# An attention and two-layer mixer kernel whose first token tile gets a written-out order

## Chip, cores and metric

The kernel runs on one core of one Trainium2 chip. The metric is the device time of one execution in microseconds; the time of a kernel is the median of its runs.

## The reference

Attention over 4 batches, 8 heads and a head width of 64: 512 local queries per head see the keys within 32 positions and 32 global keys, and 32 global queries see all 544 keys. The result, 4 x 544 = 2176 tokens of width 512, passes through two layers. The first multiplies by w_in (512 x 2048), applies a piecewise function that is 0 below -1, a parabola between -1 and 1 and the identity above, and multiplies by w_out. The second multiplies the tokens by w_a and w_b (512 x 1536 each), takes the product of the two element by element and multiplies by its own w_out. Cut to what matters here:

```python
s_l = concat([scale * q_l @ k_g.T, where(|i - j| <= 32, scale * q_l @ k_l.T, -1e9)])
e = exp(s - max(s)); a = e / (sum(e) + 1e-9)
x = (a @ v).transpose(0, 2, 1, 3).reshape(tokens, 512)
h = x @ w_in
g = where(h >= 1, h, where(h <= -1, 0, (h + 1) ** 2 / 4))
x = g @ w_out
out = (x @ w_a) * (x @ w_b) @ w_out2
```

## The kernel before

Tokens are cut into 17 blocks of 128 and these into six tiles t (`TILES`), of three blocks each but the last. Attention works on items: one block of 128 queries and one pair of heads p. An item loads `qk` (queries, then the keys of its window, L169) and `v` (L179). Three items make a group (`Local`, L191); in tile 0 a group is one pair p for all three blocks, so groups 0 to 3 give the four column chunks of x of that tile. A group runs through these steps:

- scores on TensorE (PE), `s_pe` L198, 24 products of 64x32 pieces into two PSUM tiles;
- mask and negated row maximum on VectorE (DVE), L215, and exp on ScalarE (ACT), L220. For tiles after the first the exp also adds up its rows;
- `norm` L223: row sums (for tile 0 by a reduction, L226), 1e-9, reciprocal of 128x6, and the six 128x128 pieces scaled, half on ScalarE (L230), half on DVE (L231);
- `t_pe` L233: transposes by a product with `ident`, copied to `pt` by ScalarE (L239);
- `v_pe` L241: 24 products with the values into `o`, copied to `xraw` by DVE (L259).

`x_chunk` (L348) splits a chunk of x into a rounded high part xh (ScalarE, L355) and the rest xl (DVE, L356). Every product of the layers is made of three: high weight by high x (L519), low weight by high x (L520), high weight by low x (L521).

`h_unit(t, f)` (L839) makes 12 such products for 128 columns f of w_in into `hp`, after which ScalarE makes r (L858) and DVE and ScalarE make g in two parts. `x_unit(t, f)` (L868) multiplies g by the rows f of w_out into four sums, two units later. h0 to h5 below are the units of tile 0 in the first stage (six of its sixteen units, `FA`); then tile 1 runs through all of its units, then tile 0 through the rest. Attention of later tiles is cut into small steps (`atoms`) that are put between the units.

Weights arrive as raw 64-bit floats (`w_load` L96, 512 KB each) and are converted: one step on ScalarE (L110), two on DVE (L111, L112), then a split on ScalarE (L119) and DVE (L120). `W1` streams them in the order i0, i1, o0, i2, o1, i3, ... (i for w_in, o for w_out). The pool `wp` has 32 slots of 4 KB per partition, shared by the first twelve `qk` and `v` tiles, the raw weights named in `EARLY` and later the converted weights; other raw tiles go through a pool of two.

The order at the start: `EARLY` fixes the loads on SP's queue (k for an item's `qk`, v for its values, w for a raw weight). Tile 0 is written as steps (`piece` L434, `tpose` L457) with filler products (`fill`, L186) between them, 54 of them, and one weight conversion behind every fifth step. The instructions of all engines are then put in order by the scheduler of the tile framework, which also places steps of later groups between those of earlier ones. During the first stage, `LEAD1` says how many weights are converted ahead of unit f.

Of the kernel before, what the change touches and what calls it, by code (L numbers as in the profile page):

```python
# [9 lines left out]
F32 = mybir.dt.float32  # L10
# [8 lines left out]
P = 128  # L19
# [33 lines left out]
START_ATOMS = 5  # L53
LEAD1 = 4

PAIRS = [(0, 1), (4, 5), (2, 3)]
NF = 12
# [12 lines left out]
def body(tc, qk, vw, kg, vg, vt, w1i, w1o, w2a, w2b, w2o, mask, eye, out):  # L70
# [10 lines left out]
    ident = cp.tile([P, P], F32, name="ident")  # L81
    half = cp.tile([P, 1], F32, name="half")
    nc.gpsimd.memset(half, 0.5)
    masks = ap.tile([P, 3, P], BF16, name="masks", bufs=1)

    def f32(t):
# [104 lines left out]
    class Local:  # L191
        def __init__(self, t, members):
            self.t = t
            self.tag = "h" if t else "acc"
            self.items = members
            self.nt = len(members)

# [8 lines left out]
                                         start=True, stop=True, tile_position=(64 * h, WIN * a))  # L206

        def s_post(self):
            self.e = ap.tile([P, 3, 2, P], F32, name="e", tag="e", bufs=EBUFS)
            mn = ap.tile([P, 3, 2], F32, name="mn", tag="mn", bufs=EBUFS)  # L210
            self.sm = ap.tile([P, 3, 2], F32, name="sm", tag="sm", bufs=EBUFS)
            for n, it in enumerate(self.items):
                m = 1 if it.i == 0 else (2 if it.i == SL // P - 1 else 0)
                for h in range(2):
                    nc.vector.tensor_tensor_reduce(  # L215
                        self.e[:, n, h], self.s[h][:, n], masks[:, m], -SCALE, 3.0e38, ALU.add, ALU.min,
                        mn[:, n, h:h + 1])
                for h in range(2):
                    acc = self.sm[:, n, h:h + 1] if self.t else None
                    nc.scalar.activation(self.e[:, n, h], self.e[:, n, h], AF.Exp, bias=mn[:, n, h:h + 1],  # L220
                                         scale=-1.0, accum_out=acc)

        def norm(self):  # L223
            sm = self.sm[:, :self.nt]
            if not self.t:
                nc.vector.tensor_reduce(sm, self.e[:, :self.nt], mybir.AxisListType.X, ALU.add)  # L226
            nc.vector.tensor_scalar_add(sm, sm, 1e-9)
            nc.vector.reciprocal(sm, sm)
            for n in range(self.nt):
                nc.scalar.activation(self.e[:, n, 0], self.e[:, n, 0], AF.Copy, scale=self.sm[:, n, 0:1])  # L230
                nc.vector.tensor_scalar_mul(self.e[:, n, 1], self.e[:, n, 1], self.sm[:, n, 1:2])  # L231

        def t_pe(self, n):  # L233
            it = self.items[n]
            tp = ps.tile([P, 2, P], F32, name="tp", tag=self.tag)
            for h in range(2):
                nc.tensor.transpose(tp[:, h], self.e[:, n, h], ident)
            it.pt = ap.tile([P, 2, P], F32, name="pt", tag="pt", bufs=PTBUFS)
            nc.scalar.activation(it.pt, tp, AF.Copy)  # L239

        def v_pe(self):  # L241
            self.o = ps.tile([P, self.nt * P], F32, name="o", tag=self.tag)
            for n, it in enumerate(self.items):
                for a in range(NQ):
                    for h in range(2):
                        r = slice(64 * h, 64 * h + 64)
                        q0 = WIN * a
                        nc.tensor.matmul(self.o[r, n * P + q0:n * P + q0 + WIN], it.v[:, a, r],  # L248
                                         it.pt[:, h, q0:q0 + WIN], start=True, stop=True)

        def v_post(self):
# [93 lines left out]
    def widths(t):  # L345
        return P * len(TILES[t])
# [86 lines left out]

    def piece(gs, gv):  # L434
        def run():
            if gs == 0:
                for kind in EARLY:
                    {"k": load_k, "v": load_v, "w": lambda: W1.load_to(W1.li + 1)}[kind]()
            else:
                loads()  # L440
            if gs is not None:
                if gs > START_GROUPS:
                    groups[gs - 1].norm()
                s_part(groups[gs])
            if gv is not None:
                v_part(groups[gv])
            if 0 < (gs or 0) < START_GROUPS:
                fill(WARM_S)
            if gv is not None:
                groups[gv].v_post()  # L450
                if groups[gv].t == 0:
                    x_chunk(0, groups[gv].items[0].p, widths(0))
            if gs is not None:
                groups[gs].s_post()
        return run

    def tpose(g, n):  # L457
        def run():
            loads()
            if n == 0 and (g < START_GROUPS or g == len(groups) - 1):  # L460
                groups[g].norm()
            groups[g].t_pe(n)
            if g < START_GROUPS:
                fill(WARM_T)
        return run

    atoms = [piece(0, None), piece(1, None)]
    ends = {}
    ns = 2
    for g, grp in enumerate(groups):  # L470
        n = grp.nt if isinstance(grp, Local) else 1
        atoms += [tpose(g, i) for i in range(n)]
        hold = g == START_GROUPS - 2
        atoms.append(piece(None if hold or ns >= len(groups) else ns, g))
        ns += not hold
        if grp.t >= 0:
            ends[grp.t] = len(atoms)
        if g == START_GROUPS - 1:
            atoms.append(piece(ns, None))
            ns += 1  # L480
    ends[len(TILES) - 1] = len(atoms)
    done = {"n": 0}

# [346 lines left out]
    ws2 = [(("y", f2), w2o[f2]) for f2 in range(NF2)]  # L830
# [75 lines left out]
    for u in range(len(units)):  # L906
        for kind in (0, 1):
            if kind == 0:
# [362 lines left out]
```

## Time and profile before

| | |
|---|---|
| median of 3 runs | 901.22 us (901.16 to 906.14) |
| profiled execution | 902.52 us, its span 900.7 us |
| granted clock of TensorE, mean | 0.996 |
| busy share of the span | PE 98%, DVE 70%, ACT 54% |
| moved by DMA | 153.61 MB, mean 171 GB/s |

The span runs from the first to the last instruction of the profiled execution; 1.8 us lie around it. Times in the rows count from the span's start. PE is the matrix engine's products, PEld its weight loads; a product of two 32-bit operands stands as two passes (x2) where its operands are not of the rounded type. Busy PE includes fillers. "Granted clock" 1.00 is 2.4 GHz.

### The profile page before, as it was taken

How to read it: one execution, taken by the hardware profiler on the slowest of the kernel's cores; microseconds unless marked ns; L12 is line 12 of the kernel's file. 1: busy time of each engine (PE TensorE's matmuls, PEld its weight loads, DVE VectorE, ACT ScalarE, POOL GpSimd, SP SyncE). 2: the span in 40 equal slices, each digit the busy share in tenths (PEclk: the TensorE clock that was granted, in tenths of full speed). 3: DMA queues.
4: the chain of work that ended last, by engine and by line, in shares of the span. 5: the costliest groups of instructions: out<-in, count | busy, mean ns of one | idle time of the engine just before them, and what ended most of it. 6: DMA issues, size and time to landing. Idle time of an engine off the chain costs nothing.

```text
span 900.7 us, 19419 instructions
## 1 busy us (share of the span) xinstructions
PE 884.2 (98%) x7382; PEld 837.8 (93%) x7382; DVE 634.3 (70%) x1587; ACT 489.2 (54%) x1192; POOL 0.3 (0%) x5
## 2 busy tenths in 40 slices
PE   8999998999999999999999999999999999999998
PEld 7889997999999999988999999999988999999998
DVE  5779897666566655555489687776987568676683
ACT  5869675555455444443456555555755446555442
POOL 0000000000000000000000000000000000000000
PEclk9999999999999999999999999999999999999999
DMA  9787566755543532344283454432788421644521
GB/s 324 241 280 259 179 217 220 268 180 187 161 139 131 173 113 90 121 146 150 74 283 85 149 194 155 164 118 109 245 293 278 152 82 42 200 136 132 198 102 54
DMA packets 82413, 153.61 MB, mean 171 GB/s; under 512 B 9488, under 2 KB 40592, under 8 KB 82320
## 3 DMA queue, kind: packets, MB, share of 16 engines
q1 hardware_dynamic: 81744, 151.85, 51.5%
q8 instruction: 58, 0.95, 0.4%
q10 hardware_dynamic: 576, 0.52, 0.2%
q14 instruction: 35, 0.29, 0.1%
HBM read 119.05 MB, written 33.29 MB: 169 GB/s over the span
## 4 chain that ended last, share of the span: by engine, by line
PE 84%; DMA 7%; DVE 4%; ACT 3%; issue 1%; SPq 0%; ACTq 0%; DVEq 0%
PE hp L519 6%; PE acc L519 6%; PE hp L521 6%; PE hp L520 6%; PE acc L520 6%; PE acc L521 6%; PE pb L712 4%; PE pb L714 4%; PE pb L715 4%; PE o L248 3%; PE px L712 3%; PE py L779 3%; PE px L714 3%; PE px L715 3%; PE py L780 3%; PE py L778 3%
## 5 line engine op out<-in xcount | busy, mean ns | idle before, releaser
L519 PE MATMUL hp<-xh,w 128*128 128x384 f32 (+1 forms) x384 | 132.2, 344 | 4.4 <-ACT pt L239 1.7
L519 PE MATMUL acc<-g,w 128*128 128x384 f32 (+1 forms) x384 | 127.7, 333 | 0.0
L521 PE MATMUL hp<-xl,w 128*128 128x384 f32 (+1 forms) x384 | 126.4, 330 | 0.4 <-DMA xl<-x0d 0.4
L520 PE MATMUL hp<-xh,w 128*128 128x384 f32 (+1 forms) x384 | 126.2, 329 | 0.0
L520 PE MATMUL acc<-g,w 128*128 128x384 f32 (+1 forms) x384 | 125.7, 327 | 0.0
L521 PE MATMUL acc<-g,w 128*128 128x384 f32 (+1 forms) x384 | 125.7, 327 | 0.0
L859 DVE SCALAR_TENSOR_TENSOR m<-hp,r 128x384 f32<-128x384 f32 (+1 forms) x96 | 51.2, 533 | 85.5 <-ACT r L858 85.3
L858 ACT ACTIVATE r<-hp,half 128x384 f32<-128x384 f32 (+1 forms) x96 | 53.9, 561 | 89.8 <-PE hp L521 86.5
L863 ACT ACTIVATE g<-m 128x384 fp32r<-128x384 f32 (+1 forms) x96 | 48.4, 504 | 58.6 <-DVE m L860 58.5
L519 PEld LDWEIGHTS hp<-xh,w 128*128 128x128 f32 x384 | 72.8, 190 | 7.0 <-ACT pt L239 2.0
L712 PE MATMUL pb<-w 128*128 128x384 f32 (+1 forms) x240 | 78.1, 325 | 1.2 <-ACT r L751 0.6
L119 ACT ACTIVATE w<-wt 128x512 fp32r<-128x512 f32 (+1 forms) x94 | 53.6, 571 | 46.4 <-PE pb L715 27.5
L714 PE MATMUL pb<-w 128*128 128x384 f32 (+1 forms) x240 | 78.2, 326 | 0.0
L715 PE MATMUL pb<-w 128*128 128x384 f32 (+1 forms) x240 | 78.0, 325 | 0.0
L521 PEld LDWEIGHTS hp<-xl,w 128*128 128x128 f32 x384 | 72.8, 190 | 1.3 <-DMA xl<-x0d 1.0
L519 PEld LDWEIGHTS acc<-g,w 128*128 128x128 f32 x384 | 72.4, 188 | 0.9
L520 PEld LDWEIGHTS hp<-xh,w 128*128 128x128 f32 x384 | 73.1, 190 | 0.0
L521 PEld LDWEIGHTS acc<-g,w 128*128 128x128 f32 x384 | 72.4, 188 | 0.2
L520 PEld LDWEIGHTS acc<-g,w 128*128 128x128 f32 x384 | 72.4, 189 | 0.0
L864 DVE TENSOR_TENSOR g<-m,g 128x384 fp32r<-128x384 f32 (+1 forms) x96 | 51.1, 533 | 22.4 <-ACT g L863 22.2
L120 DVE TENSOR_TENSOR w<-wt,w 128x512 fp32r<-128x512 f32 (+1 forms) x94 | 57.8, 617 | 4.0 <-ACT w L119 2.9
L220 ACT ACTIVATE e<-e,mn 128x128 f32<-128x128 f32 x128 | 48.0, 394 | 13.1 <-DVE mn L215 13.1
(169 smaller groups left out, 2063.0 us busy)
## 6 DMA issues: line engine op xcount, KB each, us to landing
v<-in_vw_dram SPq DMA_DIRECT2D x64, 256.0 KB, 5.2
wt<-wd SPq DMA_DIRECT2D x50, 256.0 KB, 2.9
qk<-in_qk_dram SPq DMA_DIRECT2D x62, 176.0 KB, 4.2
wraw<-in_w1i_dram SPq DMA_DIRECT2D x16, 512.0 KB, 4.9
wraw<-in_w1o_dram SPq DMA_DIRECT2D x16, 512.0 KB, 4.4
wraw<-in_w2a_dram SPq DMA_DIRECT2D x12, 512.0 KB, 4.3
wraw<-in_w2b_dram SPq DMA_DIRECT2D x12, 512.0 KB, 3.7
wd<-wt SPq DMA_DIRECT2D x24, 256.0 KB, 2.3
```

The costliest lines, as they stand in the source:

```text
L119: nc.scalar.activation(hi, src, AF.Copy)
L120: nc.vector.tensor_tensor(lo, src, f32(hi), ALU.subtract)
L519: nc.tensor.matmul(acc, whi, xhi, start=first, stop=False)
L520: nc.tensor.matmul(acc, wlo, xhi, start=False, stop=False)
L521: nc.tensor.matmul(acc, whi, xlo, start=False, stop=last)
L712: nc.tensor.matmul(out[:, :n], w[:, 0, r], hi[:, c, :n], start=start and c == 0, stop=False, skip_group_check=True)
L714: nc.tensor.matmul(out[:, :n], w[:, 1, r], hi[:, c, :n], start=False, stop=False, skip_group_check=True)
L715: nc.tensor.matmul(out[:, :n], w[:, 0, r], lo[:, c, :n], start=False, stop=k in (1, 5, 6) and c == 1, skip_group_check=True)
L858: at["act"] = nc.scalar.activation(r[:, :W], hp[:, :W], AF.Relu, bias=half, scale=0.5 / W_UP).ins
L859: nc.vector.scalar_tensor_tensor(m[:, :W], hp[:, :W], 1.0 / W_UP, r[:, :W], ALU.mult, ALU.max)
L863: nc.scalar.activation(gh[:, :W], m[:, :W], AF.Copy)
L864: nc.vector.tensor_tensor(gl[:, :W], m[:, :W], f32(gh[:, :W]), ALU.subtract)
```

## The change

Tile 0 leaves the steps and is written out in `begin`. Under `in_order` each of PE, ScalarE and DVE runs its instructions of `begin` in the order in which they are written; SP is not bound. The rows of a group are no longer scaled before the transposes. Instead, six products of `pt` with a tile of ones give each column's sum in the layout of `o` (`z`), and `v_post` adds 1e-9, takes the reciprocal of 128x384 and multiplies `o` by it. The fillers go from 54 to 16. `EARLY` is longer: two more key tiles, five more value tiles and four more raw weights, so that eight raw weights lie in slots of `wp`. Conversions of three weights are spread over groups 1 to 3 (`w_begin`, `w_end`). `LEAD1` is 3 instead of 4, and the conversions of the first stage are `paced`, that is, put behind the last h unit's r and g on ScalarE and DVE.

```diff
-WARM_S, WARM_T = 6, 3
+WARM = 4
-EARLY = "kkkkkkkkkvvvkkkwvvvwvvvwkkkvvvw"
+EARLY = "kkkkkkkkkvvvkkkwvvvwvvvwkkkvvvwkkvvvwwvvww"
-LEAD1 = 4
+LEAD1 = 3
...
         def norm(self):
             sm = self.sm[:, :self.nt]
-            if not self.t:
-                nc.vector.tensor_reduce(sm, self.e[:, :self.nt], mybir.AxisListType.X, ALU.add)
...
         def v_pe(self):
-            self.o = ps.tile([P, self.nt * P], F32, name="o", tag=self.tag)
+            self.o = ps.tile([P, self.nt * P], F32, name="o", tag="h")
...
+            if not self.t:
+                self.z = ps.tile([P, self.nt * P], F32, name="z", tag="h")
+                for n, it in enumerate(self.items):
+                    for h in range(2):
+                        nc.tensor.matmul(self.z[64 * h:64 * h + 64, n * P:(n + 1) * P], ones, it.pt[:, h],
+                                         start=True, stop=True)
...
         def v_post(self):
...
-                nc.vector.tensor_copy(xraw_cur[self.t][it.p][:, it.j * P:(it.j + w) * P],
-                                      self.o[:, n * P:(n + w) * P])
+                x = xraw_cur[self.t][it.p][:, it.j * P:(it.j + w) * P]
+                c = slice(n * P, (n + w) * P)
+                if self.t:
+                    nc.vector.tensor_copy(x, self.o[:, c])
+                else:
+                    z = mp.tile([P, 384], F32, name="zs", tag="r", bufs=3)
+                    nc.vector.tensor_scalar_add(z, self.z[:, c], 1e-9)
+                    nc.vector.reciprocal(z, z)
+                    nc.vector.tensor_tensor(x, self.o[:, c], z, ALU.mult)
...
+    def w_begin():
+        pend.append(w_conv())
+        W1.si += 1
+        W1.load_to(W1.si + sp["raw"])
+
+    def w_end():
+        key, tf = pend.pop(0)
+        w = slot()
+        split(w[:, 0], w[:, 1], tf)
+        wslots[key] = w
...
+    def begin():
+        for kind in EARLY:
+            {"k": load_k, "v": load_v, "w": lambda: W1.load_to(W1.li + 1)}[kind]()
+        n = START_GROUPS
+        s_part(groups[0])
+        groups[0].s_post()
+        s_part(groups[1])
+        fill(WARM)
+        for g in range(n):
+            for i in range(3):
+                groups[g].t_pe(i)
+                if g + 1 < n:
+                    groups[g + 1].post(i)
+            if g + 2 < n:
+                s_part(groups[g + 2])
+            if pend:
+                w_end()
+            v_part(groups[g])
+            if g + 1 < n:
+                fill(WARM)
+            else:
+                s_part(groups[n])
+            groups[g].v_post()
+            x_chunk(0, g, widths(0))
+            if g:
+                w_begin()
+        groups[n].s_post()
+        while pend:
+            w_end()
...
-    att_step(10 ** 9)
-    k = 0
-    while att_step(ends[0]):
-        k += 1
-        if k % START_ATOMS == 0:
-            W1.step()
+    with in_order():
+        begin()
...
                     while W1.si < min(2 * f + LEAD1, n1):
-                        W1.step()
+                        paced(W1.step)
                 if si == 1:
-                    want = max(n1 + (len(ws1) - n1) * (f + 1) // (NF1 - 3), 2 * f + LEAD1)
+                    want = max(n1 + (len(ws1) - n1) * (f + 1) // (NF1 - 3), 2 * f + LEAD1 + 1)
```

What stands on the engines at three places (a row: line, operation, tile written <- tiles read, shape, count). First ScalarE in tile 0, between the splits of chunk 0 (`xh0`) and chunk 1 (`xh1`); in the kernel before `e_439` and `e_560` belong to groups 2 and 3, `pt_473` to `pt_491` to group 1:

```order
L355 ACTIVATE xh0_435<-xraw0_398 128x384
L220 ACTIVATE e_439<-e_439,mn_440 128x128
L239 ACTIVATE pt_473<-tp_470 128x256
L239 ACTIVATE pt_482<-tp_479 128x256
L239 ACTIVATE pt_491<-tp_488 128x256
L230 ACTIVATE e_439<-e_439,sm_441 128x128 x3
L110 ACTIVATE wt_675<-wraw0_217 128x512
L220 ACTIVATE e_560<-e_560,mn_561 128x128 x5
L355 ACTIVATE xh1_556<-xraw1_399 128x384
```

In the changed kernel, the same stretch; `pt_437` to `pt_458` belong to group 1, `e_439` to group 2, `wt_535` is the first weight:

```order
L371 ACTIVATE xh0_430<-xraw0_385 128x384
L242 ACTIVATE pt_437<-tp_434 128x256
L225 ACTIVATE e_439<-e_439,mn_440 128x128 x2
L242 ACTIVATE pt_449<-tp_446 128x256
L225 ACTIVATE e_439<-e_439,mn_440 128x128 x2
L242 ACTIVATE pt_458<-tp_455 128x256
L225 ACTIVATE e_439<-e_439,mn_440 128x128 x2
L371 ACTIVATE xh1_531<-xraw1_386 128x384
L111 ACTIVATE wt_535<-wraw0_203 128x512
```

The scalings (L230) are gone, and exp and copies alternate behind xh0; the next xh stands directly behind them, with the conversion of a weight behind it.

Second, DVE in tile 0. Before, from the copy of group 0's `o` on (`sm_441` are the row sums of group 2):

```order
L259 COPY xraw0_398<-o_402 128x384
L215 ISA e_439,mn_440<-s1_373,masks_75 128x128
L215 ISA mn_440 128x1
L111 TENSOR_SCALAR wt_593<-wt_593 128x512
L356 TENSOR_TENSOR xl0_436<-xraw0_398,xh0_435 128x384
L226 TENSOR_REDUCE sm_441<-e_439 128x6
L112 SCALAR_TENSOR_TENSOR wt_593<-wraw0_209,wt_593 128x512
L227 TENSOR_SCALAR sm_441<-sm_441 128x6
L228 RECIPROCAL sm_441<-sm_441 128x6
L231 TENSOR_SCALAR e_439<-e_439,sm_441 128x128 x3
```

In the changed kernel, from the sums of group 1 on (`e_544` are the masks of group 3):

```order
L274 TENSOR_SCALAR zs_527<-z_515 128x384
L275 RECIPROCAL zs_527<-zs_527 128x384
L276 TENSOR_TENSOR xraw1_386<-o_490,zs_527 128x384
L372 TENSOR_TENSOR xl1_532<-xraw1_386,xh1_531 128x384
L112 TENSOR_SCALAR wt_535<-wt_535 128x512
L113 SCALAR_TENSOR_TENSOR wt_535<-wraw0_203,wt_535 128x512
L220 ISA e_544,mn_545<-s0_464,masks_77 128x128
```

The copy became three instructions (L274 to L276), and they, xl and two steps of a conversion (L112, L113) stand ahead of the next group's masks, which stood ahead of the copy before.

Third, ScalarE around r of unit h0 (`r_786` before, `r_740` now). Before:

```order
L110 ACTIVATE wt_843<-wraw_682 128x512
L110 ACTIVATE wt_852<-wraw_771 128x512
L858 ACTIVATE r_786<-hp_773,half_73 128x384
L230 ACTIVATE e_749<-e_749,sm_751 128x128 x3
L220 ACTIVATE e_828,sm_830<-e_828,mn_829 128x128
L863 ACTIVATE g_788<-m_787 128x384
L220 ACTIVATE e_828,sm_830<-e_828,mn_829 128x128 x5
L119 ACTIVATE w_847<-wt_843 128x512
L119 ACTIVATE w_856<-wt_852 128x512
L858 ACTIVATE r_876<-hp_861,half_73 128x384
```

In the changed kernel, where `wt_797` and `w_801` are the weight of h2:

```order
L111 ACTIVATE wt_705<-wraw0_219 128x512
L913 ACTIVATE r_740<-hp_727,half_73 128x384
L111 ACTIVATE wt_797<-wraw0_233 128x512
L111 ACTIVATE wt_804<-wraw0_245 128x512
L225 ACTIVATE e_709,sm_711<-e_709,mn_710 128x128 x6
L120 ACTIVATE w_724<-wt_705 128x512
L225 ACTIVATE e_782,sm_784<-e_782,mn_783 128x128
L233 ACTIVATE e_709<-e_709,sm_711 128x128 x3
L225 ACTIVATE e_782,sm_784<-e_782,mn_783 128x128 x5
L120 ACTIVATE w_801<-wt_797 128x512
L120 ACTIVATE w_808<-wt_804 128x512
L918 ACTIVATE g_742<-m_741 128x384
```

The weight of h2 was converted ahead of r before; `w_847` and `w_856` there are for later units. Now its conversion begins behind r, and twelve exp of groups 4 and 5 with three scalings stand between that and its split. Before, six of those twelve exp stood ahead of r.

On SP's queue the third key tile of group 5 (`qk_746`), which the end of h0 has to wait for in PE's row, now stands behind two more raw weights and six stores of x0 (`x0_store` L498), of which the last reads xl2.

## Rows read from the trace of the kernel before

**Rows 1.** The page's busy table: busy us (share of span) xinstructions of each engine.

```profile
PE 884.2 (98%) x7382; PEld 837.8 (93%) x7382; DVE 634.3 (70%) x1587; ACT 489.2 (54%) x1192; POOL 0.3 (0%) x5
```

**Rows 2.** Timeline of PE: start, us, engine line op out<-in xcount [idle before <-releaser].

```profile
12.28 0.80 PE L205 MATMUL s<-qk 64*32 64x128 f32 x20 [2.81 <-DMA qk<-in_qk_dram]
...
44.38 0.42 PE L519 MATMUL hp<-xh,w 128*128 128x384 f32 x1
...
53.85 0.64 PE L519 MATMUL hp<-xh,w 128*128 128x384 f32 x1 [1.70 <-ACT pt L239]
...
63.06 0.44 PE L519 MATMUL hp<-xh,w 128*128 128x384 f32 x1
```

**Rows 3.** The chain that ended last, 0 to 60 us: start us, us, what.

```profile
16.82 0.67 PE warm L189 x6
17.49 1.52 PE o L248 x48
...
35.88 1.52 PE o L248 x48
...
37.77 0.17 PE hp L520
...
54.49 0.32 PE hp L520
```

**Rows 4.** Timeline of ScalarE (ACT), columns as in rows 2.

```profile
6.21 3.62 ACT L220 ACTIVATE e<-e,mn 128x128 f32<-128x128 f32 x12 [2.31 <-DVE mn L215]
...
40.88 0.58 ACT L858 ACTIVATE r<-hp,half 128x384 f32<-128x384 f32 x1 [0.66 <-PE hp L521]
41.35 0.97 ACT L230 ACTIVATE e<-e,sm 128x128 f32<-128x128 f32 x3
```

**Rows 5.** Windows of 5 us: length, busy by engine, granted clock, DMA share, GB/s.

```profile
10.00:15.00 5.00, 2.72 (x30) 2.46 (x31) 2.21 (x8) 1.61 (x5) 0.00 (x0) 0.80 0.96 316
...
20.00:25.00 5.00, 5.00 (x101) 4.68 (x100) 4.27 (x19) 3.60 (x12) 0.00 (x0) 1.00 1.04 367
```

**Rows 6.** Tile v: two issues on SP (6.0 to 7.5 us), and landing.

```profile
L184 SPq DMA_DIRECT2D v<-in_vw_dram x2: 328/379/430, 6.1 to 6.5; - x2
...
DMA to landing us min/median/max: 4.9/5.1/5.2
```

**Rows 7.** Groups of DVE by shape: names, shapes, count, busy us, mean ns, idle.

```profile
L112 DVE SCALAR_TENSOR_TENSOR wt<-wraw,wt 128x512 int32<-128x512 int32 x68 | 46.8, 689 | 1.2
...
L215 DVE CUSTOM_DVE_ANT_0 e<-s,masks 128x128 f32<-128x128 f32 x128 | 30.0, 286 | 7.3 <-PE s L205 7.0 <-PE tp L237 0.3
L111 DVE TENSOR_SCALAR wt<-wt 128x512 int32<-128x512 int32 x68 | 28.7, 423 | 15.3 <-ACT wt L110 15.3
...
L887 DVE TENSOR_SCALAR x<-acc 128x384 f32<-128x384 f32 x10 | 5.5, 555 | 2.3 <-PE acc L521 2.2
...
L228 DVE RECIPROCAL sm<-sm 128x6 f32<-128x6 f32 x20 | 3.8, 190 | 0.6
...
L227 DVE TENSOR_SCALAR sm<-sm 128x6 f32<-128x6 f32 x20 | 3.4, 170 | 7.8 <-ACT e L220 7.7
...
L228 DVE RECIPROCAL sm<-sm 128x4 f32<-128x4 f32 x2 | 0.4, 178 | 0.1
L227 DVE TENSOR_SCALAR sm<-sm 128x4 f32<-128x4 f32 x2 | 0.3, 171 | 0.4 <-ACT e L220 0.4
```

**Rows 8.** Groups of ScalarE by shape, columns as in rows 7.

```profile
L220 ACT ACTIVATE e<-e,mn 128x128 f32<-128x128 f32 x128 | 48.0, 394 | 13.1 <-DVE mn L215 13.1
...
L110 ACT ACTIVATE wt<-wraw 128x512 f32<-128x512 f32 x68 | 45.0, 665 | 16.4 <-DMA wraw<-in_w1o_dram 7.6 <-DVE w L120 7.0 <-DMA wraw<-in_w1i_dram 1.7
L119 ACT ACTIVATE w<-wt 128x512 fp32r<-128x512 f32 x69 | 43.2, 628 | 18.9 <-DVE wt L112 11.1 <-PE px L715 6.4 <-PE acc L521 0.9
...
L239 ACT ACTIVATE pt<-tp 128x256 f32<-128x256 f32 x64 | 24.0, 378 | 6.6 <-PE tp L237 6.2 <-ACT w L119 0.3
...
L355 ACT ACTIVATE xh<-xraw 128x384 fp32r<-128x384 f32 x20 | 10.5, 526 | 1.9 <-DVE xraw L259 1.8
```

More of the change, by code (lines that the diff above doesn't have):

```diff
@@ L83, in body @@
     nc.gpsimd.memset(half, 0.5)
+    ones = cp.tile([P, D], F32, name="ones")
+    nc.gpsimd.memset(ones, 1.0)
     masks = ap.tile([P, 3, P], BF16, name="masks", bufs=1)
@@ L193, in __init__ @@
             self.t = t
-            self.tag = "h" if t else "acc"
             self.items = members
@@ L208, in s_post, with post @@
         def s_post(self):
[L209 to L221, printed above, removed]
+            for n in range(self.nt):
+                self.post(n)
+        def post(self, n):
+            if n == 0:
+                self.e = ap.tile([P, 3, 2, P], F32, name="e", tag="e", bufs=EBUFS)
+                self.mn = ap.tile([P, 3, 2], F32, name="mn", tag="mn", bufs=EBUFS)
+                self.sm = ap.tile([P, 3, 2], F32, name="sm", tag="sm", bufs=EBUFS)
+            i = self.items[n].i
+            m = 1 if i == 0 else (2 if i == SL // P - 1 else 0)
+            for h in range(2):
+                nc.vector.tensor_tensor_reduce(
+                    self.e[:, n, h], self.s[h][:, n], masks[:, m], -SCALE, 3.0e38, ALU.add, ALU.min,
+                    self.mn[:, n, h:h + 1])
+            for h in range(2):
+                acc = self.sm[:, n, h:h + 1] if self.t else None
+                nc.scalar.activation(self.e[:, n, h], self.e[:, n, h], AF.Exp, bias=self.mn[:, n, h:h + 1],
+                                     scale=-1.0, accum_out=acc)
         def norm(self):
             sm = self.sm[:, :self.nt]
-            if not self.t:
-                nc.vector.tensor_reduce(sm, self.e[:, :self.nt], mybir.AxisListType.X, ALU.add)
             nc.vector.tensor_scalar_add(sm, sm, 1e-9)
@@ L234, in t_pe @@
             it = self.items[n]
-            tp = ps.tile([P, 2, P], F32, name="tp", tag=self.tag)
+            tp = ps.tile([P, 2, P], F32, name="tp", tag="h" if self.t else "acc")
             for h in range(2):
@@ L249, in v_pe @@
                                          it.pt[:, h, q0:q0 + WIN], start=True, stop=True)
+            if not self.t:
+                self.z = ps.tile([P, self.nt * P], F32, name="z", tag="h")
+                for n, it in enumerate(self.items):
+                    for h in range(2):
+                        nc.tensor.matmul(self.z[64 * h:64 * h + 64, n * P:(n + 1) * P], ones, it.pt[:, h],
+                                         start=True, stop=True)
         def v_post(self):
@@ L435, in run @@
         def run():
[L436 to L440, printed above, removed]
+            loads()
             if gs is not None:
-                if gs > START_GROUPS:
-                    groups[gs - 1].norm()
+                groups[gs - 1].norm()
                 s_part(groups[gs])
@@ L459, in run @@
             loads()
-            if n == 0 and (g < START_GROUPS or g == len(groups) - 1):
+            if n == 0 and g == len(groups) - 1:
                 groups[g].norm()
             groups[g].t_pe(n)
-            if g < START_GROUPS:
-                fill(WARM_T)
-        return run
-    atoms = [piece(0, None), piece(1, None)]
-    ends = {}
-    ns = 2
+        return run
+    pend = []
+    def w_begin():
+        pend.append(w_conv())
+        W1.si += 1
+        W1.load_to(W1.si + sp["raw"])
@@ new lines, in w_end, with in_order @@
+    def w_end():
[3 more added lines that the diff above has]
+        wslots[key] = w
+    @contextlib.contextmanager
+    def in_order():
+        traced = nc.cur_bb.bb.instructions
+        n0 = len(traced)
+        yield
+        last = {}
+        for i in traced[n0:]:
+            if i.engine in (mybir.EngineType.PE, mybir.EngineType.Activation, mybir.EngineType.DVE):
+                if i.engine in last:
+                    tc.add_manual_dep(
+                        i, last[i.engine].name,
+                        mybir.DependencyInfo(mybir.DependencyClass.NoSync, mybir.DependencyReason.DATA),
+                        reason="in_order")
+                last[i.engine] = i
@@ L470, in body @@
+    atoms = [piece(START_GROUPS + 1, None)]
+    ends = {0: 0}
+    ns = START_GROUPS + 2
     for g, grp in enumerate(groups):
+        if g < START_GROUPS:
+            continue
         n = grp.nt if isinstance(grp, Local) else 1
         atoms += [tpose(g, i) for i in range(n)]
-        hold = g == START_GROUPS - 2
-        atoms.append(piece(None if hold or ns >= len(groups) else ns, g))
-        ns += not hold
+        atoms.append(piece(ns if ns < len(groups) else None, g))
+        ns += 1
```

9 lines of the change are left out of this document (removed).

## Prediction

> **What bounds the kernel now.** The page's busy table comes first [rows 1]: TensorE (PE) is busy for 98% of the span, so a change pays only where PE waits or does work that could be left out. PE's timeline and the chain of waits place that at the start. PE waits 2.81 us up to 12.28 for a transfer of keys [rows 2]. By their place these are the keys of group 3, and yet they hold up the transposes of group 0, which stand behind them in PE's row. From then on the products with one group's values start every (35.88 - 17.49)/3 = 6.13 us [rows 3]. A step of that loop holds 15 filler products; six passes (three fillers) take 0.67, so 15 take 3.35: the step is made of fillers and waits, not of needed work. ScalarE's r, which reads the finished unit h0, starts at 40.88 [rows 4]. Behind it, PE idles 1.70 before h3 at 53.85 [rows 2], and its products then follow 0.32 apart, against 0.17 at 37.77 [rows 3]. That is half the clock after an idle stretch; likewise the granted clock of 10 to 15 us is 0.80, around the wait of 2.81 [rows 5]. The lower of its two levels (1.2 GHz of 2.4) holds for about ten products there: 10 x 0.15 = 1.5 us lost. h4 starts at 63.06. What follows h4 is the same work in both kernels, so the change is worth what it does to the start of h4.
>
> **The change part by part.** I follow one chain: end of a group's sums (z), scaled x, next group's z.
>
> Start. The third value tile of group 0 is issued at 6.5 and lands 4.9 later, at 11.4 [rows 6]. The transposes no longer stand behind group 3's keys and are done by then. Two thirds of the 1.52 us of value products are left at 11.4 and end at 12.4. The sums are 6 products of two 128-column passes; a filler pass of that width takes 0.67/6 = 0.11 [rows 3], so z takes 1.33 and ends at 13.7. Value products of the same 128x64 shape take 1.52/48 = 0.032 for 32 columns, no less per column than a filler, so I count no overlap of the two halves. (The Trainium skill, "TensorEngine Tiling (Array Packing)", section Key Properties, says that different tiles of the array can work at the same time; by it z would take 0.67 and the sum would be 4 x 0.67 = 2.7 less. The value products of this trace do not show it.)
>
> Scaling. Three dependent VectorE (DVE) instructions replace a copy: an add out of PSUM (555 ns for 128x384), a reciprocal of 128x384, a product (taken as 555), 0.03 between them. No row shows a wide reciprocal; call its time R. From below: if it streams like its neighbours, R = 0.55. From above: from 4 to 6 elements it grows by 190 - 178 = 12 ns, while TENSOR_SCALAR on the same tile goes from 171 to 170 [rows 7]; over that it stands 7 and then 20 ns higher, 6.5 more per element. For 384: 0.555 + 0.020 + 378 x 0.0065 = 3.03. I take R = 3.03, the only row of this operation that grows with length; the scaling is 0.56 + 3.03 + 0.56 + 0.1 = 4.25. (The Trainium skill, "VectorE: DVE Perf Modes", section First, the fixed hardware budget, describes the reciprocal as an iterated divide with a repeat count of 8. At that page's 0.96 GHz this gives an estimate of 8 x 384/960 = 3.2, and a sum 0.7 higher.)
>
> From scaled x to the next z. In ScalarE's new row xh stands ahead of the next group's pt copies, and in DVE's row the scaling, xl and a weight conversion stand ahead of the next masks, so each group waits for the one before. With xh 0.53, pt 0.38, conversion 0.67 on ScalarE [rows 8] and 0.42 + 0.69 on DVE, mask steps 0.29 [rows 7], and exp 0.30 apart (3.62 for 12) [rows 4]:
> x0 to z1: xh 0.53, xl 0.5, five mask steps 1.43 (they free the PSUM slot), values 1.52, z 1.33: 5.3.
> x1 to z2: xh and conversion 1.13, DVE's two conversion steps 1.15, a mask step, two exp, pt, two exp, pt 2.2, last third of the values 0.5, z 1.33: 6.3.
> x2 to z3: xh and conversion 1.03, first pt 0.4, values 1.52, z 1.33: 4.3.
> Scaled x3 is ready at 13.7 + 4 x 4.25 + 5.3 + 6.3 + 4.3 = 46.6. With xh 0.55, xl 0.58 and the last product 0.33, h0 ends at 48.1 instead of 40.9: 7.2 later. What the change takes out does not lie on this path: four reductions, 24 scalings by row sums and 38 of 54 fillers go, but they stood beside, or ahead of, a chain that is now longer. h0 ends at 48.1 + 4(R - 3.03), level with before at R = 1.2.
>
> h0 to h4. Eight raw tiles lie in SBUF early, so the wait for raw weights before h3 goes. But LEAD1 is lower by one and conversions are paced behind r of h0. ScalarE's row between r and the weight of h2 now holds two conversions 1.14, 6 + 1 + 5 exp with sums at 0.39, an L120 at 0.52 and three scalings 0.97; with r 0.47 that is 7.8. The two splits of the weight add 0.63 and 0.69, and h2 starts 9.3 after r, against 44.38 - 40.88 = 3.5 before. The exps of group 4, whose scores are there, cannot pass r in that row. The work from h2 to h4 is the same: 63.06 - 44.38 = 18.7 before, of it 1.7 idle and 1.5 for the low clock, so 15.5. Two products of x0 that stood ahead of h2 come behind it (0.35), and h2 starts at half the clock after its wait (1.5). h4 then starts 9.3 + 15.5 + 0.35 + 1.5 = 26.6 after r, against 22.2: 4.4 more.
>
> Clock in tile 0. Around x of each group PE idles about 2 us twice. I count the half clock in one of the three legs: z 1.33 and a third of the values 0.5 take twice as long, 1.8. It could be none or all three (0 to 5.4).
>
> Behind h4 I count nothing: the conversions stand at the same units as before and hide behind PE's products. If the new order of loads uncovers one of them, it costs at most about 1 us.
>
> Sum: 7.2 + 4.4 + 1.8 = 13.4. The profiled execution took 902.5 (span 900.7), so 915.9; the median of the runs shown is 901.2, 1.3 below it, so I forecast 914.5.
>
> **The rivals.** First, on the other side: R is about 0.55, as for DVE's other instructions of that width. Then x3 is ready at 36.7 and h0 could end at 38.1. It may be held by a transfer: the third key tile of group 5 stands in SP's row behind two more raw tiles and six stores of x0; 14.3 MB lie before and in it, and at 367 GB/s [rows 5] they take 39 us, so h0 ends at 38.1 to 41. If the stall before h2 shrinks with the masks that come earlier (0 to 4.4), the median comes to 899 to 906, no change. For it: every other row of that width. Against it: the growth from 4 to 6 elements. Up to R near 2 the kernel is not slower by 1%.
> Second: the half clock holds in all three legs and in all of their value products: 3.6 + 3 x 1 more, 918 to 921. For it: the clock fell after 1.9 and 2.8 us without work. Against it: 16 fillers still stand between z and the transposes.
> Third: the exps run in time for h2, 4.4 goes and the stall before h3 is gone with it (1.7 + 1.5): 907 to 911. Against it: the rows' order on ScalarE.
>
> **How the numbers follow.** Forecast 0.45 (911 to 917 by itself), first rival 0.27, second 0.18, third 0.10. A measurement of this kernel can tell about 1%, 9 us, from no change, so the line lies at 910.2. Slower by more: all of the forecast but 0.04, all of the second, 0.02 of the third: 0.61. Faster by more: 0.03 of the first, 0.01 elsewhere: 0.04. The rest, 0.35, is within 1%. The range 901 to 920 leaves out a tenth on each side.
>
> **What the profile of the changed kernel would show.** The reciprocal's row for 128x384 at about 3 us bears the chain out; 0.55 ends it, and the forecast with it. r of h0 should start near 48 (38 to 41 by the first rival), the value products of groups 1 to 3 9 to 11 us after one another. Between r and the weight of h2 ScalarE should be busy for 8 us while PE idles about 6. The wait for raw weights before h3 should be gone. The forecast is wrong if r of h0 starts before 43, or if h4 starts less than 24 us behind it.

## The result, and the profile after the change

| | before | after |
|---|---|---|
| median | 902.64 us (8 runs, 900.27 to 906.14) | 912.57 us (8 runs, 908.91 to 915.06) |
| ratio, 95% interval | 1 | 1.0098 (1.0073 to 1.0124) |
| profiled execution, span | 902.52, 900.7 us | 909.59, 907.7 us |
| mean granted clock | 0.996 | 0.989 |

The changed kernel is slower by 1.0%, 9 us. The runs of the kernel before in this table were made beside those of the changed kernel. The profiled execution of the changed kernel is the second quickest of its eight, so the two traces differ by only 7.0 us of span. I follow the difference through the program with these two.

The page's busy table after the change [rows 1]:

```profile
PE 887.1 (98%) x7354; PEld 838.3 (92%) x7354; DVE 639.8 (70%) x1571; ACT 485.8 (54%) x1180; POOL 0.4 (0%) x6
```

PE runs 28 instructions fewer and is busy 2.9 us longer; the half clock shown below lengthens its products. The other 4.1 us of the longer span are idle time of PE. The table does not show where the loss arises; the timelines do. Next the groups of DVE by shape in the first 60 us (names, shapes, count, busy us, mean ns, idle) [rows 7]:

```profile
L275 DVE RECIPROCAL zs<-zs 128x384 f32<-128x384 f32 x4 | 10.2, 2553 | 0.1
...
L274 DVE TENSOR_SCALAR zs<-z 128x384 f32<-128x384 f32 x4 | 2.2, 558 | 9.8 <-PE z L257 9.8
L276 DVE TENSOR_TENSOR xraw<-o,zs 128x384 f32<-128x384 f32 x4 | 2.2, 557 | 0.1
...
L231 DVE RECIPROCAL sm<-sm 128x6 f32<-128x6 f32 x2 | 0.4, 188 | 0.0
```

The wide reciprocal takes 2.55 us, 4.6 times its neighbours of the same width. DVE's timeline shows where the scalings stand (start, us, instruction, idle before and its releaser):

```profile
13.83 0.56 DVE L274 TENSOR_SCALAR zs<-z 128x384 f32<-128x384 f32 x1 [4.36 <-PE z L257]
...
17.01 0.56 DVE L276 TENSOR_TENSOR xraw<-o,zs 128x384 f32<-128x384 f32 x1
...
23.77 0.56 DVE L274 TENSOR_SCALAR zs<-z 128x384 f32<-128x384 f32 x1 [3.79 <-PE z L257]
...
34.38 0.56 DVE L274 TENSOR_SCALAR zs<-z 128x384 f32<-128x384 f32 x1 [0.68 <-PE z L257]
...
42.82 0.56 DVE L274 TENSOR_SCALAR zs<-z 128x384 f32<-128x384 f32 x1 [1.02 <-PE z L257]
...
46.00 0.56 DVE L276 TENSOR_TENSOR xraw<-o,zs 128x384 f32<-128x384 f32 x1
```

This is the chain: the sums of a group end (13.83), x is scaled 3.74 later (17.01 + 0.56), and only then does the next group get on. PE's timeline shows the other half of it [rows 2, 3]:

```profile
12.92 0.85 PE L257 MATMUL z<-pt,ones 128*64 128x128 f32 x12
...
17.62 0.92 PE L205 MATMUL s<-qk 64*32 64x128 f32 x46 [1.76 <-DVE xraw L276]
19.87 2.55 PE L251 MATMUL o<-pt,v 128*64 128x32 f32 x48 [1.33 <-ACT e L225]
...
28.95 0.66 PE L251 MATMUL o<-pt,v 128*64 128x32 f32 x16 [3.47 <-ACT pt L242]
31.07 1.92 PE L251 MATMUL o<-pt,v 128*64 128x32 f32 x32 [1.46 <-ACT pt L242]
32.80 1.53 PE L257 MATMUL z<-pt,ones 128*64 128x128 f32 x12
...
39.55 1.90 PE L251 MATMUL o<-pt,v 128*64 128x32 f32 x48 [2.06 <-ACT pt L242]
...
48.05 0.44 PE L581 MATMUL hp<-xl,w 128*128 128x384 f32 x1
...
56.86 0.44 PE L579 MATMUL hp<-xh,w 128*128 128x384 f32 x1 [1.64 <-ACT w L120]
...
73.58 0.44 PE L579 MATMUL hp<-xh,w 128*128 128x384 f32 x1
```

PE waits for x, for exps and for pt, by turns, and its value products start 8.4, 9.1 and 10.6 us after one another, where they stood 6.13 apart. The last product of h0 ends at 48.49 (48.05 + 0.44). h2 starts at 56.86, held by the split of its weight; h4 starts at 73.58. ScalarE's timeline around r of h0 [rows 4]:

```profile
46.59 0.52 ACT L371 ACTIVATE xh<-xraw 128x384 fp32r<-128x384 f32 x1 [5.51 <-DVE xraw L276]
...
48.60 0.58 ACT L913 ACTIVATE r<-hp,half 128x384 f32<-128x384 f32 x1 [0.91 <-PE hp L581]
49.08 1.20 ACT L111 ACTIVATE wt<-wraw 128x512 f32<-128x512 f32 x2
50.17 0.39 ACT L225 ACTIVATE e<-e,mn 128x128 f32<-128x128 f32 x1
...
56.20 1.14 ACT L120 ACTIVATE w<-wt 128x512 fp32r<-128x512 f32 x2
```

ScalarE stands idle for 5.5 us up to xh, then works without a gap from 48.60 to 58. The windows show the clock (length, busy of PE, PEld, DVE, ACT and POOL, granted clock, DMA share, GB/s) [rows 5]:

```profile
17.60:18.50 0.90, 0.88 (x46) 0.66 (x46) 0.34 (x1) 0.80 (x2) 0.00 (x0) 1.00 1.06 410
...
20.00:25.00 5.00, 5.00 (x72) 4.68 (x72) 1.19 (x2) 1.35 (x5) 0.00 (x0) 0.66 1.01 377
25.00:30.00 5.00, 1.14 (x21) 0.79 (x19) 4.34 (x8) 1.35 (x3) 0.00 (x0) 1.00 1.02 383
...
28.90:29.60 0.70, 0.65 (x16) 0.55 (x16) 0.67 (x2) 0.00 (x0) 0.00 (x0) 1.00 1.06 404
...
30.00:35.00 5.00, 3.93 (x47) 3.60 (x48) 2.36 (x15) 2.91 (x9) 0.00 (x0) 0.54 1.03 403
35.00:40.00 5.00, 2.94 (x29) 2.66 (x27) 4.34 (x5) 1.85 (x5) 0.00 (x0) 0.78 0.78 293
40.00:45.00 5.00, 5.00 (x105) 4.31 (x102) 3.25 (x4) 0.67 (x2) 0.00 (x0) 0.66 0.45 152
```

All three legs (a leg goes from the scaled x of one group to the end of the next group's z) have a stretch at half the clock; in windows of half a microsecond these run from about 20.2 to 23.5, 30.4 to 37.2 and 40.7 to 44.0 us. An idle stretch alone does not bring it: the work that follows idle times of 1.76 us (at 17.62) and 3.47 us (at 28.95) is still granted 1.00.

Last, what lies behind h4. Taking the start of the same unit in both traces, the lag is 11.6 us at every h unit from h8 to h18. Then it shrinks. These are rows of PE's timeline of the kernel before, late in the first stages and at 670 us:

```profile
140.05 0.44 PE L519 MATMUL hp<-xh,w 128*128 128x384 f32 x1 [0.63 <-DVE m L859]
...
145.72 0.44 PE L519 MATMUL hp<-xh,w 128*128 128x384 f32 x1 [1.22 <-DVE xraw L259]
...
156.06 0.44 PE L521 MATMUL hp<-xl,w 128*128 128x384 f32 x1 [0.40 <-DMA xl<-x0d]
...
157.34 0.44 PE L519 MATMUL hp<-xh,w 128*128 128x384 f32 x1 [0.84 <-DMA xh<-x0d]
...
669.85 0.42 PE L712 MATMUL px<-w,w 128*128 128x320 f32 x1 [1.50 <-DVE m L752]
```

and of the changed kernel, the same units h19 and h20:

```profile
150.96 0.44 PE L579 MATMUL hp<-xh,w 128*128 128x384 f32 x1
...
155.22 0.33 PE L579 MATMUL hp<-xh,w 128*128 128x384 f32 x1
```

The kernel before waits at these places and the later one does not, or hardly: the lag falls to 10.9 (h19), 9.5 (h20), 8.9 (h23), 7.6 behind 669.85 and 7.0 at the end. So in this pair of executions 11.6 us were lost up to h8 and 4.6 came back.

### The profile page after: what moved, and what is told of

The parts are those of the page before. It is cut to its first block, busy times and chain, and to the rows that moved or that the text cites. A ratio compares the mean times of both kernels' runs of the same rounds, so it can differ in the third digit from the quotient of the medians.

```text
span 907.7 us, 19339 instructions
## 1 busy us (share of the span) xinstructions
PE 887.1 (98%) x7354; PEld 838.3 (92%) x7354; DVE 639.8 (70%) x1571; ACT 485.8 (54%) x1180; POOL 0.4 (0%) x6
## 4 chain that ended last, share of the span: by engine, by line
PE 87%; DMA 7%; DVE 3%; ACT 2%; issue 1%; SPq 0%; ACTq 0%; DVEq 0%
PE hp L579 7%; PE acc L579 7%; PE hp L580 7%; PE hp L581 7%; PE acc L581 7%; PE acc L580 7%; PE pb L772 4%; PE pb L774 4%; PE pb L775 4%; PE px L772 3%; PE py L839 3%; PE px L774 3%; PE px L775 3%; PE py L840 3%; PE py L838 3%; PE o L251 3%
## 5 line engine op out<-in xcount | busy, mean ns | idle before, releaser
L914 DVE SCALAR_TENSOR_TENSOR m<-hp,r 128x384 f32<-128x384 f32 (+1 forms) x96 | 51.1, 532 | 83.8 <-ACT r L913 83.7
```

Of the source, the lines that this page charges most:

```text
L914: nc.vector.scalar_tensor_tensor(m[:, :W], hp[:, :W], 1.0 / W_UP, r[:, :W], ALU.mult, ALU.max)
```

## The experiments

All twelve, with their median, the ratio to the kernel before as run beside them on the same chip (95% interval), and two marks of their traces: r of h0, and the later of the starts of h7 and x5. The second mark is used because h4 stands ahead of x2 in some kernels and behind it in others. The marks belong to one profiled execution each, which for 3, 7 and 11 is the slowest of its runs. In 1, 2, 6, 7, 9 and 10 r of h0 is not released by the end of h0: it starts directly behind group 4's exps and one or two splits in ScalarE's row.

| kernel | us | ratio | r of h0 | h7, x5 |
|---|---|---|---|---|
| before | 902.64 | 1 | 40.88 | 83.8 |
| after | 912.57 | 1.0098 (1.0073 to 1.0124) | 48.60 | 95.4 |
| 1 reciprocal left out | 903.89 | 1.0000 (0.9983 to 1.0017) | 39.97 | 84.2 |
| 2 sums from the exps | 901.79 | 0.9976 (0.9956 to 0.9996) | 39.34 | 81.7 |
| 3 old conversion rule | 909.22 | 1.0075 (1.0045 to 1.0105) | 48.57 | 97.2 |
| 4 short list of loads | 912.53 | 1.0099 (1.0071 to 1.0127) | 48.73 | 95.6 |
| 5 = 2, short list | 904.16 | 1.0028 (1.0007 to 1.0049) | 35.96 | 87.2 |
| 6 = 2, more fillers | 902.56 | 0.9986 (0.9970 to 1.0003) | 40.85 | 84.5 |
| 7 = 2, old rule | 899.16 | 0.9976 (0.9956 to 0.9996) | 40.13 | 86.6 |
| 8 after, more fillers | 908.51 | 1.0068 (1.0047 to 1.0089) | 46.01 | 92.3 |
| 9 = 2, key tile earlier | 897.15 | 0.9946 (0.9925 to 0.9967) | 39.38 | 82.4 |
| 10 = 7, key tile earlier | 901.97 | 1.0004 (0.9985 to 1.0022) | 39.71 | 84.7 |
| 11 after, exps of group 4 first | 910.81 | 1.0105 (1.0085 to 1.0126) | 52.53 | 94.2 |
| 12 before, new loads and rule | 900.78 | 0.9985 (0.9970 to 1.0001) | 43.87 | 84.5 |

**1. The reciprocal alone.** My theory was the serial chain; the rival, that the written order and the clock cost the time.

```diff
-                    nc.vector.reciprocal(z, z)
```

> This kernel leaves out the reciprocal in the scaling of tile 0 (x becomes o times the sum), so its x is not the reference's. Chain theory: the four reciprocals of 2.55 us stand one behind the other on the path to h0, so r of h0 comes 8 to 10.2 us earlier than 48.6, at 38.4 to 40.6; h4 stays about 25 us behind r, and the time falls from 912.6 to 903 to 905. Rival (the written order and the half clock cost the time, the reciprocals lie mostly beside other work): r of h0 not before 44, time 908 to 911.

r of h0 comes 8.6 us earlier, at 39.97, and the ratio falls from 1.0098 to 1.0000. The chain theory holds, and the rival, as an account of the whole loss, falls. The chain itself got shorter than r tells. These rows are from the timelines of DVE, PE and ScalarE (ACT) of this kernel:

```profile
34.01 0.56 DVE L275 TENSOR_TENSOR xraw<-o,zs 128x384 f32<-128x384 f32 x1
...
36.19 0.34 PE L580 MATMUL hp<-xl,w 128*128 128x384 f32 x1
...
39.97 0.56 ACT L912 ACTIVATE r<-hp,half 128x384 f32<-128x384 f32 x1
```

x3 is scaled at 34.57 instead of 46.56, and h0 ends at 36.53 instead of 48.49: 12.0 us earlier, where four reciprocals with their gaps make 10.3. Of the other 1.7, 1.1 came in the first leg, where less was run at half the clock (its value products took 1.61 us instead of 2.55), 0.3 ahead of it and 0.2 in the third leg. r then stands behind group 4's exps, which gives 3.4 of the 12.0 back at once; that it fell into my 38.4 to 40.6 is in part luck. A wait that the chain had covered also appears (PE's timeline of this kernel, group 5's scores, which stand behind h0 and ahead of h1):

```profile
41.68 1.63 PE L205 MATMUL s<-qk 64*32 64x128 f32 x32 [4.58 <-DMA qk<-in_qk_dram]
```

This is the third key tile of group 5, which stands in SP's row behind raw weights and the stores of x0. It holds up h1, not the end of h0.

**2. The other way to the sums.** The written order stays; the sums come free with the exps, and e is scaled ahead of the transposes.

```diff
-                acc = self.sm[:, n, h:h + 1] if self.t else None
+                acc = self.sm[:, n, h:h + 1]
...
         groups[0].s_post()
+        groups[0].norm()
...
+            if g + 1 < n:
+                groups[g + 1].norm()
             if g + 2 < n:
...
-            if not self.t:
+            if False:
                 self.z = ps.tile(...)
...
-                if self.t:
+                if True:
                     nc.vector.tensor_copy(x, self.o[:, c])
```

> The written order stays, but the sums come from the exps' accumulators as in later tiles, and e is scaled ahead of the transposes (two steps on 128x6, three scalings on each of two engines per group); no products with ones, no wide reciprocal. Chain theory: per group 0.56 + 2.55 + 0.03 and 0.85 to 1.5 of z go from the path, at most 4 x 4.4 = 17.6; ScalarE's row (three pt 0.38, six exps 0.39, three scalings 0.33, xh 0.53, a conversion 0.67, a split 0.57: 6.2 per group) then bounds the step, so r of h0 at 35 to 40 and 900 to 905 us. Rival (the written order itself is what costs): r of h0 stays above 44 and the time above 908.

901.8 us, 0.9976 of before: as the chain theory said, r of h0 at 39.3. The written order with these sums costs nothing; with run 1, this leaves the wide reciprocal as the cost. In its place one on 128x6 (0.19 us) stands ahead of the group's transposes, off the way from one group's products to the next group's. The same wait for keys is left, 1.7 us:

```profile
41.09 0.45 PE L205 MATMUL s<-qk 64*32 64x128 f32 x16 [1.69 <-DMA qk<-in_qk_dram]
```

**3. The conversion rule.**

```diff
-LEAD1 = 3
+LEAD1 = 4
...
-                        paced(W1.step)
+                        W1.step()
...
-... 2 * f + LEAD1 + 1)
+... 2 * f + LEAD1)
```

> The rule for the first weight conversions is that of the kernel before (lead of four, not paced behind r); the rest is the changed kernel. If the weight's place in ScalarE's row is what holds h2 (8.3 us behind r instead of 3.5): h2 starts 3.5 to 5 behind r, h4 22 to 23 behind r instead of 25.0, time 909 to 911. Rival (group 4's exps and scalings must run then anyway, and h3 or h4 waits in place of h2): h4 24 to 25.5 behind r, time 912 to 913.

Inconclusive. The median is 3 us lower, but the interval overlaps that of the changed kernel, and the profiled execution, one of its slowest at 914.9 us, has h2 8.0 us behind r (8.3 after the change) and h4 25.9 behind it. The median lies in the 909 to 911 that I gave for the old rule, but the early start of h2 that was to bring it did not come.

**4. The loads.**

```diff
-EARLY = "kkkkkkkkkvvvkkkwvvvwvvvwkkkvvvwkkvvvwwvvww"
+EARLY = "kkkkkkkkkvvvkkkwvvvwvvvwkkkvvvw"
```

> The early list of loads is cut to that of the kernel before (31 items, four raw weight tiles); the rest is the changed kernel. If the raw tiles give back the 3 us behind h4 (the stalls that the kernel before had between 140 and 158 us): stalls of 2 to 3 us come back there, and one of about 1.7 ahead of h3 or h4, time 915 to 918. Rival (the stalls went because the later groups' work stands further ahead of the units, whatever the loads): nothing comes back behind h4, time 912 to 915.

No change (1.0099). The eight raw tiles are worth nothing measurable to the changed kernel, and PE does not wait ahead of h3 or h4 without them. Waits of 1.42 and 0.57 us, the 2 us that my first theory named, do stand behind h4 in this trace; the larger is

```profile
152.95 0.45 PE L579 MATMUL hp<-xh,w 128*128 128x384 f32 x1 [1.42 <-DVE m L914]
```

The time did not rise with them, so the raw tiles are not shown to be what gives the time back there, nor excluded.

**5. The loads, without the chain.** The edit of 4 on kernel 2.

> The kernel with sums from the exps' accumulators (901.8 us), with the early list of loads cut to that of the kernel before (four raw weight tiles). If the raw tiles delay group 5's keys: the wait of 1.7 us for keys at 41 us goes, h4 comes 1 to 2 us earlier, 899.5 to 901 us. Rival (a wait for raw weights before h3 or at a conversion takes its place): 901 to 903.5 us, and a DMA-bound idle time ahead of h3 of 1 us or more.

The rival's time came true, by more than it said: 1.0028 against 0.9976. Its cause, a wait for transfers ahead of h3, did not. The wait for keys falls to 0.27 and r of h0 comes at 35.96, the earliest of all, but then PE waits for g, which stands in ScalarE's row behind twelve exps, a split, three scalings and two conversions (36.43 to 43.56):

```profile
44.12 0.69 PE L582 MATMUL acc<-g,w 128*128 128x384 f32 x1 [2.64 <-ACT g L921]
```

So the long list is worth 0.5% where the chain is short, and nothing measurable where it is long (run 4).

**6 and 8. The clock.** More fillers behind the first three groups' products, in kernel 2 (14) and in the changed kernel (16).

```diff
             if g + 1 < n:
-                fill(WARM)
+                fill(16)
```

> The kernel with sums from the exps' accumulators, with 14 fillers behind each of the first three groups' value products in place of 4. If half clock costs time there (the clock was 0.5 from 25 to 37 us): the clock of 25 to 35 us comes to 0.9 or more, r of h0 1 to 3 us earlier than 39.3, 899 to 901.5 us. Rival (the 20 passes more per group, 2.2 to 2.9 us, stand on the path): r of h0 at 40.5 to 43, 903 to 906 us.

> The changed kernel with 16 fillers behind each of the first three groups' sums in place of 4. If the half clock in the three legs stands on the path (values 0.8 and z 0.65 longer per leg than at full clock): the clock of 20 to 45 us comes to 0.9 or more, r of h0 at 44 to 46 instead of 48.6, 908 to 910 us. Rivals: the clock is low all the same or costs nothing, r within 1 us of 48.6, 911.5 to 913.5 us; or the fillers (24 passes more, 2.6 to 3.5 us per leg) push the transposes and all behind them back, r after 50, 914 us or more.

In the changed kernel r of h0 comes 2.6 us earlier and the later mark 3.0; the ratio is 1.0068 against 1.0098, whose intervals still overlap a little. The second leg keeps half the clock, the others do not:

```profile
20.00:25.00 5.00, 5.00 (x67) 4.83 (x64) 3.56 (x3) 0.52 (x2) 0.00 (x0) 1.00 1.05 388
25.00:30.00 5.00, 2.74 (x49) 2.39 (x47) 3.06 (x16) 3.70 (x12) 0.00 (x0) 0.81 1.05 398
30.00:35.00 5.00, 5.00 (x39) 4.67 (x38) 3.68 (x3) 0.57 (x2) 0.00 (x0) 0.51 1.04 401
35.00:40.00 5.00, 4.90 (x85) 4.61 (x84) 3.04 (x6) 2.54 (x6) 0.00 (x0) 1.00 0.92 350
```

By these two traces the half clock stood on the path, with about these 2.6 us net of what the fillers cost. In kernel 2 the fillers lift the clock too (from 0.50 to 0.82 and 0.84 between 25 and 35 us), and h0 ends 0.8 us earlier; but x3 is ready 1.5 us later, group 4's masks and exps with it, and so r of h0, which stands behind them. The wait for keys grows to 2.72 us, and the time, between the two ranges that I gave, is not told apart from kernel 2's: the fillers cost what they save.

**7, 9 and 10. Towards a better kernel.** 7 is kernel 2 with the edit of 3. 9 gives the awaited key tile a place in the early list, ahead of the fifth raw weight, and 10 is 9 with the edit of 3.

```diff
-EARLY = "kkkkkkkkkvvvkkkwvvvwvvvwkkkvvvwkkvvvwwvvww"
+EARLY = "kkkkkkkkkvvvkkkwvvvwvvvwkkkvvvwkkkvvvwvvww"
+EARLY_K = 13
...
-            if n < EARLY_ITEMS:
+            if n < EARLY_K:
...
-        return n < max(EARLY_ITEMS, ld["s_done"]) + QKBUFS
+        return n < max(EARLY_K, ld["s_done"]) + QKBUFS
```

> The kernel with sums from the exps' accumulators, with the rule for the first weight conversions of the kernel before (lead of four, not paced). If that rule is worth the 3 us by which it lay lower on the changed kernel: 898 to 900 us. Rival (that difference lay within what the runs scatter, or it only stood in for a stall that this kernel has not): 901 to 903 us.

> The kernel with sums from the exps' accumulators, and the third key tile of group 5 gets a place of its own in the early list, ahead of the fifth raw weight (thirteen keys and seven raw weights in the early slots in place of twelve and eight). If the wait for that tile (1.7 us at 41 us) is on the path: it goes, and the time falls by 1 to 2 us against 0.9976 of the kernel before, to 0.995 to 0.9965. Rival (ScalarE's row behind r of h0 takes its place, as its row was busy without a gap from 40 to 45 us): 0.997 to 0.999.

> As e9_norm_key, with the first weight conversions by the rule of the kernel before. There the wait for keys was 3.6 us, so if it is on the path 2 to 3 us go: 0.994 to 0.996 of the kernel before. Rival: ScalarE's row takes its place, 0.997 to 0.999.

7 has the ratio of 2 to the fourth digit: the conversion rule gains nothing there, although its median lies in the 898 to 900 that I gave for a gain. 9 has the lowest time of the study, 897.15 us, 0.54% below the kernel before and by the ratios 1.5% below the changed one; the wait for keys is gone. Its interval still overlaps those of 2 and 7 a little, so that it is faster than they are is likely and not shown. 10, with weights converted sooner, loses that again (intervals apart), and lies above both ranges that I gave for it. ScalarE's timelines show where the two part. Kernel 9, then kernel 10:

```profile
39.38 0.56 ACT L917 ACTIVATE r<-hp,half 128x384 f32<-128x384 f32 x1
39.84 0.98 ACT L234 ACTIVATE e<-e,sm 128x128 f32<-128x128 f32 x3
```

```profile
39.71 0.56 ACT L917 ACTIVATE r<-hp,half 128x384 f32<-128x384 f32 x1
40.17 0.62 ACT L121 ACTIVATE w<-wt 128x512 fp32r<-128x512 f32 x1
40.69 1.20 ACT L112 ACTIVATE wt<-wraw 128x512 f32<-128x512 f32 x2
41.80 0.97 ACT L234 ACTIVATE e<-e,sm 128x128 f32<-128x128 f32 x3
```

Conversions go ahead of group 4's scalings, and PE waits for those scalings (PE's timeline of kernel 10):

```profile
42.24 0.44 PE L241 MATMUL tp<-ident,e 128*128 128x128 f32 x2 [1.75 <-ACT e L234]
```

That is part of the difference; what makes up the rest is not shown. I had held the lower lead for a cost; in kernel 9 it is a gain of 0.6%.

**11. The exps behind r.**

```diff
                 s_part(groups[n])
+                groups[n].s_post()
             groups[g].v_post()
...
-        groups[n].s_post()
         while pend:
```

> The changed kernel with the masks and exps of group 4 written ahead of the scaling of group 3 in place of behind it. They wait for group 4's scores, so x of group 3 and r of h0 come 1.5 to 2.5 us later (50 to 51). If the exps that stand behind r of h0 in ScalarE's row make the way from r to h4 longer (25.0 against 22.2 us before): it falls to 22 to 23.3, and the time stays at 911 to 913. Rival (they do not): r to h4 stays at 24.5 to 25.5, and the time rises to 914 to 916.

r of h0 comes 3.9 later (52.53), and h4 20.9 behind it instead of 25.0, with x2 now ahead of h4; both move by more than I said. So the exps behind r are what made that way long. The time stays: 1.0105 against 1.0098. In these traces the work of ScalarE and DVE is paid on either side of r.

**12. The rest of the change on the kernel before.** The long list and the new conversion rule, with its own tile 0.

> The kernel before with only the change's loads and conversion rule (long early list, lead of three, first conversions paced); tile 0 is its own. If the sums of tile 0 carry the whole loss: within 2 us of the kernel before (0.998 to 1.002). Rival (the later weight conversions cost the 2.8 us between r of h0 and h4): 1.002 to 1.005.

0.9985 (0.9970 to 1.0001): within what I gave for "the sums carry the whole loss". The loads and the rule do move something: r of h0 comes 3.0 later, at 43.87, since the first product of h0 waits for the split of its weight:

```profile
38.28 0.69 PE L519 MATMUL hp<-xh,w 128*128 128x384 f32 x1 [2.25 <-ACT w L119]
```

But at the later mark only 0.7 us of it are left. With run 1 this closes the account: the loss is in tile 0's scaling, not in the loads or the conversions.

## Why the prediction was right, point by point

The forecast was 914.5, the median is 912.6. The mechanism was right: the sums' wide reciprocal, four times on one serial chain, delays h0, and the new order on ScalarE delays h2 behind it. The sizes were less good than the 1.9 us between these two times suggest. I added 13.4 us to the kernel before; the medians are 9.9 apart. 1.4 of the excess is hidden by luck, because the eight runs of the kernel before beside the result have a median of 902.6 and the three that I started from had 901.2. The errors of the terms up to h8 add up to 1.8 too much (13.4 against a lag of 11.6); the rest is what came back behind.

**Start.** z of group 0 was to end at 13.7 and ended at 13.8. Two errors cancel here. The value products came later: all 48, not two thirds, ran from 11.50, and z began at 12.92, not 12.4. And z took 0.85 us, not 1.33: "I count no overlap of the two halves" was wrong. A filler pass took 0.12 at full clock (32 in 3.84 us, run 8), a z pass 0.07. This fits two halves that overlap in part; a z pass also has weights of half the width, and no run separates the two. The Trainium skill, "TensorEngine Tiling (Array Packing)", section Key Properties, says that different tiles can work at the same time; z's 0.07 a pass against 0.12 is in line with that, and the page was the better guide than the value products that I took for proof against it. The half clock hid this in the other groups (1.53 to 1.56 a time).

**Scaling.** The step "I take R = 3.03" was 0.48 too high: R is 2.55, and a scaling takes 3.74, not 4.25. Over four groups that is 2.0 us too much. The growth from 4 to 6 elements was the right sign to follow (6 ns each); what was wrong was to add all of it to the 0.555 of a neighbour. From the row of 128x6 alone, 0.190 + 378 x 0.006 would have given 2.46. The Trainium skill, "VectorE: DVE Perf Modes", section First, the fixed hardware budget, with its repeat count of 8, gave an estimate of 3.2; the measurement is 20% below it.

**The legs.** From scaled x to the end of the next z I had 5.3, 6.3 and 4.3, and 1.8 for the clock in one of them: 17.7. Measured, from the DVE rows above: 23.77 - 17.57 = 6.2, 34.38 - 27.51 = 6.9, 42.82 - 38.11 = 4.7: 17.8. The sum is right by two errors that cancel: the clock fell in all three legs, as my second rival said, but z is shorter than I took it to be at full clock and costs only 0.2 more than that at half. x3 was ready at 46.56 and r of h0 started at 48.60, 2.0 behind it where I had 1.5. That is 7.7 later than before, where I had 7.2 and 1.8.

**h0 to h4.** I said that h2 would start 9.3 behind r and h4 26.6 (the terms of the first sum make 9.1). They started 8.3 and 25.0 behind it, so this term is 2.8 by the mark that I had chosen, not 4.4. The mark was not a fair one: x2 stands behind h4 now. By the lag from h8 on, 11.6, of which 7.7 were there at r, the term is 3.9. The order on ScalarE was as foretold, and run 11 shows that the exps in it are the cost; that LEAD1 has a part in it runs 3, 7 and 10 don't bear out. PE was to idle about 6 us between r and h2; it idled 2.9 (1.22 ahead of group 5's last scores and 1.64 ahead of h2), because h1 ran there, at half the clock. The wait ahead of h3 is gone, as I said, but not by the eight raw tiles: run 4, with four, has none either.

**Behind h4** I counted nothing, and this is the step that failed: 4.6 us came back in the profiled pair. Beside the medians, which are 9.9 us apart, it is about 2; the ratio of 1.0098 makes it nearer 3. Waits of the kernel before are missing or shorter in the later one. Why is open: that a kernel that comes later finds a wait over is a guess, and run 4, just as late, still waits 1.42 and 0.57 us.

**The rivals.** The first needed R near 0.55. Run 1, with no reciprocal at all, came to 903.9, inside its 899 to 906. The transfer that the rival named was waited for there, but it held h1; the end of h0 came at 36.5, ahead of the rival's 38.1 to 41. The second rival's clock came true and its 918 to 921 did not: R was 0.48 shorter each time, z cost less than I had counted, and part of the lag came back. The third, exps in time for h2, did not happen.

## What to carry to other kernels

Before a row sum is turned into products with ones, look at what follows it: a cheap sum that ends in a wide reciprocal on the path costs more than a narrow reciprocal ahead of it (2.55 against 0.19 us here), the more so where the next group stands behind it in a fixed order. When a stall is removed, read which transfer or row was covered by it: here 4.6 us of waiting for keys stood behind the 10 us of reciprocals, and moving one tile forward in the loads gave the lowest time of the study. Look also at what releases the mark that you measure by: r of h0 stood behind other work of ScalarE as soon as h0 was early. A lag at the start isn't what is left at the end; here 4.6 of 11.6 us came back at waits further on, for reasons that stay open.

## What the runs showed of the hardware

The reciprocal takes longer with each element of a row, by about 6.25 ns from 128x6 (0.19 us) to 128x384 (2.55 us), while every other DVE instruction of that shape in these traces took 0.55 to 0.56. Two halves of 64 columns of weights with 128 columns of data each took 0.85 us for 12 passes at the granted clock of 1.00 and 1.53 at half of it. The granted clock stayed at 1.00 in work right behind 1.76 and 3.47 us without products, and fell later.
